# Queries and keys of ten of eighteen tiles turned by 32x32 squares on VectorE instead of by TensorE

## The chip, the cores and the metric

The kernel runs on one NeuronCore of a Trainium2 chip. The metric is the device time of one execution in microseconds (us), lower is better. The engines are written as the profile writes them: PE is TensorE (PEld its weight loads), DVE VectorE, ACT ScalarE, POOL GpSimd and SP SyncE, which here only issues DMAs.

## The reference

Three stages run one after the other on 2304 tokens (4 batches of 576), all in float32: sliding-window attention with 8 heads of 64 and a window of 64 keys, a gated layer of width 1536, and a soft mixture of 8 experts with 4 slots each.

```python
scores = (q @ k.T) / sqrt(64);  keep 0 <= i - j < 64          # per batch and head
x = softmax(scores) @ v                                        # -> [2304, 512]
x = ((x @ w_a) * (x @ w_b)) @ w_out                            # 512 -> 1536 -> 512
logits = x @ phi                                               # 32 slots
slot_in = softmax(logits, over tokens).T @ x
slot_out[e] = relu(slot_in[e] @ w1[e]) @ w2[e]                 # 8 experts
out = softmax(logits, over slots) @ slot_out
```

## The kernel before

Tokens come in 18 tiles of 128. For each tile the attention gives x in two float32r halves (a high part and a rest), and the gated layer multiplies them with w_a and w_b in three column groups. One half of one such group, (tile, group, a or b), is a slot: 12 matmuls of 128x512 into one PSUM bank, `psa` or `psb` (line 430). There are 108 slots. ACT empties `psa` (line 437), DVE multiplies `psb` with it (line 439), and each bank has one buffer, so the next slot of the same letter needs it emptied. In the steady part a tile has six slots.

All other PE work is put between and into the slots by hand: `at(n, f, ...)` puts a function at slot n, `run_slot` runs what stands there, and PE's instructions keep that order. The order of the other engines, and of the DMAs in their queues, is set by a planner that works with times of its own; what one engine has been given runs strictly in order.

The attention of tile t (for t from 5) starts at slot s = sA[t], six slots after that of the tile before in the steady part, three or four at the end (slots 80, 83 and 86 for tiles 15 to 17). The steps that matter here:

- `load` (line 193): q and k of a tile are fetched by SP into one buffer each (tags "q" and "k"), tokens on the partitions, 512 numbers each.
- `att_q` at s - 2 (line 217): four PE transposes of 128x128 into PSUM `tq`, and one ACT copy to `qTs` that also multiplies by -SCALE (line 224). `att_k` at s - 1 (line 227): a POOL copy of the last 64 keys of the tile before (line 232), four PE transposes into `tk`, one DVE copy to `kTs` (line 243; ACT for the first five tiles, line 241). `qTs` and `kTs` hold two tiles each.
- `att_s` at s (line 245): 16 float32 matmuls of 64x64 weights (queries) by 64x128 (keys), which the trace shows as 32 pairs of load and matmul (line 258). DVE adds the mask and takes the minimum (line 271), ACT takes eight exponentials (line 278).
- `att_n` and `att_pt` at s + 1 and s + 2: DVE scales the probabilities, turns them by 32x32 squares into `pq` (line 305; tiles from 6), and POOL's DMA queue writes the squares to DRAM and reads them back in order as `pT` (lines 312 and 318).
- `att_pv` at s + 6 (line 332): 32 matmuls with v (line 346), then ACT and DVE make x (lines 349 and 351).

The product g is turned in the same way for the routing (`r_b`, line 454): DVE squares into `gq` (line 457), four writes and one read in SP's queue (lines 463 and 468), then 12 matmuls (24 pairs) at line 482. `pq` and `gq` share the three buffers of tag "e". `dps` and `ups` (lines 548 and 558) are later steps of the routing. Behind the slots comes the stage of the experts, whose weights SP fetches into memory that the attention has left.

Of the kernel before, what the change touches and what calls it, by code (L numbers as in the profile page):

```python
# [11 lines left out]
F32 = mybir.dt.float32  # L12
# [3 lines left out]
ACTF = mybir.ActivationFunctionType  # L16
# [4 lines left out]
P = 128  # L21
# [36 lines left out]
BIG = 1.0e9  # L58
HUGE = 3.0e38
# [6 lines left out]
def swa_glu_softmoe_kernel(  # L66
# [13 lines left out]
    nc = tc.nc  # L80
# [5 lines left out]
    W = 64  # L86
# [7 lines left out]
    SCALE = 1.0 / float(D) ** 0.5  # L94
    EPS = 1.0e-9
    NFIRST = 4
    NLAST = 3
    NPLAIN = NFIRST + 2
    N_EX1 = 3
    N_EX2 = 7  # L100
    EARLY = 6
# [3 lines left out]
    dram = ctx.enter_context(tc.tile_pool(name="dram", bufs=1, space=bass.MemoryType.DRAM))  # L105
# [5 lines left out]
    small = ctx.enter_context(tc.tile_pool(name="small", bufs=3))  # L111
    ex1 = ctx.enter_context(tc.tile_pool(name="ex1", bufs=N_EX1))

# [23 lines left out]
    def transpose(o, i):  # L137
        nc.tensor.transpose(o, i, ident)  # L138

    def build_ident():  # L140
        nc.gpsimd.memset(ident, 0.0)
        nc.gpsimd.affine_select(
            out=ident, in_=ident, pattern=[[-1, P]], compare_op=ALU.not_equal,
            fill=1.0, base=0, channel_multiplier=1,
        )

        nc.gpsimd.memset(masks, 0.0)
        for h in range(2):
            m = masks[W * h:W * h + W]
            nc.gpsimd.affine_select(  # L150
                out=m[:, 3], in_=m[:, 3], pattern=[[-1, W]], compare_op=ALU.is_ge,
                fill=BIG, base=0, channel_multiplier=1,
            )
            nc.gpsimd.affine_select(
                out=m[:, 0:3], in_=m[:, 0:3], pattern=[[0, 3], [1, W]], compare_op=ALU.is_gt,
                fill=BIG, base=0, channel_multiplier=-1,
            )
            nc.gpsimd.memset(m[:, 1 - h], BIG)

    def build_ri():  # L160
        nc.gpsimd.memset(ri, 0.0)
# [18 lines left out]
    att = att_stack.enter_context(tc.tile_pool(name="att", bufs=2))  # L180
# [10 lines left out]
    loaded = {}  # L191
# [19 lines left out]
    sts = {}  # L211
    xts = {}

    qTs = att.tile([P, 2, 4, P], F32, name="qTs", bufs=1)
    kTs = att.tile([P, 2, 4, W + P], F32, name="kTs", bufs=1)

    def att_q(t):
        tq = ps_t.tile([P, 4, P], F32, tag="t", name="tq")
        x = loaded[t]["q"]
        for u in range(4):  # L220
            transpose(tq[:, u], x[:, 2 * u:2 * u + 2].rearrange("p h d -> p (h d)"))
        yield
        qT = qTs[:, t % 2]
        nc.scalar.activation(out=qT, in_=tq, func=ACTF.Copy, scale=-SCALE)
        sts[t] = {"qT": qT}

    def att_k(t):
        new, old = slice(W, W + P), slice(P, P + W)
        if t == 0:
            nc.gpsimd.memset(kTs[:, 0, :, 0:W], 0.0)  # L230
        else:
            nc.gpsimd.tensor_copy(kTs[:, t % 2, :, 0:W], kTs[:, (t - 1) % 2, :, old])  # L232
        yield
        tk = ps_t.tile([P, 4, P], F32, tag="t", name="tk")
        x = loaded[t]["k"]
        for u in range(4):
            transpose(tk[:, u], x[:, 2 * u:2 * u + 2].rearrange("p h d -> p (h d)"))
        yield
        k32 = kTs[:, t % 2, :, new]
        if t <= NFIRST:  # L240
            nc.scalar.copy(out=k32, in_=tk)
        else:
            nc.vector.tensor_copy(k32, tk)  # L243

    def att_s(t):
        st = sts[t]
        qT = st["qT"]
        sm = small.tile([P, 8], F32, tag="sm", name="sm")
        nmx = small.tile([P, 8], F32, tag="nmx", name="nmx")
        st["pr"], st["sm"] = [], sm  # L250

        sps = [ps_s.tile([P, 4, P], F32, tag=f"s{h}", name=f"s{h}") for h in range(2)]
        for u in range(4):
            for h in range(2):
                r = slice(W * h, W * h + W)
                for b in range(2):
                    c = slice(W * b, W * b + W)
                    nc.tensor.matmul(  # L258
                        sps[h][c, u], lhsT=qT[r, u, c], rhs=kTs[r, t % 2, u, W * b:W * b + P],
                    )  # L260
            if u % 2:
                yield
        edge = [b for b in range(2) if (2 * t + b) % NBLK == 0]
        v = 1 - edge[0] if edge else 2
        mk = masks[:, v:4:3 - v]
        for h in range(2):
            pr = att.tile([P, 4, P], F32, tag="pr", name="pr", bufs=3)
            st["pr"].append(pr)
            for u in range(4):
                i = 4 * h + u  # L270
                nc.vector.tensor_tensor_reduce(  # L271
                    out=pr[:, u].rearrange("p (a k) -> p a k", a=2), in0=sps[h][:, u].rearrange("p (a k) -> p a k", a=2), in1=mk, scale=1.0, scalar=HUGE,
                    op0=ALU.add, op1=ALU.min, accum_out=nmx[:, i:i + 1],
                )
            yield
            for u in range(4):
                i = 4 * h + u
                nc.scalar.activation(  # L278
                    out=pr[:, u], in_=pr[:, u], func=ACTF.Exp, scale=-1.0,
                    bias=nmx[:, i:i + 1], accum_out=sm[:, i:i + 1],  # L280
                )
            yield
# [15 lines left out]
    def att_pt(t, hh):  # L298
        st = sts[t]
        if t >= NPLAIN:  # L300

# [30 lines left out]
    def att_pv(t):  # L332
        st = sts[t]
        xps = ps_t.tile([P, 4, P], F32, tag="x", name="xps", bufs=1)
        for b in range(2):
            vt = loaded[t]["b" if b else "a"]
            c = slice(W * b, W * b + W)
            for u in range(4):
                for h in range(2):
                    o = xps[W * h:W * h + W, u, c]  # L340
                    if t >= NPLAIN:
                        o = o.rearrange("p (i q) -> p i q", i=2)
# [13 lines left out]
    whi, wlo = {}, {}  # L356
    wbufs = {"w0": 8, "w1": 8, "w2": 4, "w3": 4, "e": N_EX1}
    wo_dram = dram.tile([DFF, DM], F32, name="wo_dram")
# [345 lines left out]
    def use(key):  # L704
        used.add(key)
        return exw[key]
# [11 lines left out]
    def at(n, f, *a):  # L718
        events[round(2 * n)].append((f, a))
# [6 lines left out]
    sA = {}  # L726
    for t in range(NTILE - 1, NFIRST - 1, -1):
        sA[t] = min(first[t] - (8 if t >= NPLAIN else 6), sA.get(t + 1, NSLOT) - 3)
    lastA = sA[NTILE - 1] + 7
    by_squares = [t for t in range(2, NTILE - NLAST) if done[t, NFG - 1] + 2 < lastA]  # L730
    R = {}
    for t in range(NTILE - NLAST):
        R[t] = max(done[t, NFG - 1] + (3 if t not in by_squares else 4 if t == NTILE - NLAST - 1 else 5), R[t - 1] + 4 if t else 24)
    for t in range(NFIRST, NTILE):
        s = sA[t]
        at(s, att_s, t)
        at(s + 1, att_n, t, 0)
        at(s + 1, att_n, t, 1)
        at(s + 2, att_pt, t, 0)
        late = 2 if t >= NPLAIN else 0  # L740
        at(s + 2 if late else s + 3, att_pt, t, 1)
        at(s + 4 + late, att_pv, t)
        at(s - 2, att_q, t)
        at(s - 1, att_k, t)
        if t + 1 < NTILE:
            at(s, load, t + 1, "qk")
            at(s + 5 + late, load, t + 1, "ab")
    for t in range(NTILE):
        if t < NTILE - NLAST:
            r = R[t]  # L750
# [16 lines left out]
    a, b, c = LAST  # L767
# [11 lines left out]
    def open_ex():  # L779
# [3 lines left out]
        slots.extend([(p2, "as1")] * 2 + [(p2, "gT1")] * 2)  # L783
        slots.extend([(ex1, "e")] * N_EX1 + [(exs["ex2"], "y")] * N_EX2 + [(exs["ex3"], "z")] * N_EX3 + [(gp, "g"), (xp, "x")])
        slots.extend([(wp, "w0")] * 8 + [(wp, "w1")] * 8 + [(wp, "w2")] * 4 + [(xp, "x")] + [(wp, "w3")] * 4)
        slots.extend([(xp, "x")] * 2 + [(gp, "g")] * 3)
        fetch(4 + N_EX1 + N_EX2 + N_EX3)
        for t in turns.values():
# [17 lines left out]
    def run_slot(n):  # L806
# [8 lines left out]
        for _ in pieces:  # L815
            pass

    build_ident()
    SPLIT = 6 * NFIRST
    works = {  # L820
        "Ph": lambda _: run(nc.sync.dma_start, phi, moe2_phi.rearrange("(k p) s -> p k s", p=P)), "Ri": lambda _: build_ri(),
        "Tq": lambda t: load(t, "qk"), "Tv": lambda t: load(t, "ab"), "Aq": att_q, "Ak": att_k, "As": att_s, "An": att_n,
        "Ap": att_pt, "Av": att_pv, "Sa": partial(stage_w, "a"), "Sb": partial(stage_w, "b"),
        "Da": partial(split_w, "a"), "Db": partial(split_w, "b"), "Ga": lambda t, fg: glu(t, fg, "a", "a"),
# [26 lines left out]
    sps = ps_t.tile([P, KD, NS], F32, tag="x", name="sps", bufs=1)  # L851
    with tc.manual_schedule(engines=MANUAL):
# [16 lines left out]
        for h in range(2):  # L869
            c = slice(DM // 2 * h, DM // 2 * (h + 1))  # L870
# [14 lines left out]
    for u in range(2):  # L885
        hps = [ps_ab.tile([P, 512], F32, tag="ab"[n], name=f"h{n}") for n in range(2)]
        for kk in range(KD):
            for n in range(2):
                for e in range(4):
                    nc.tensor.matmul(  # L890
                        hps[n][32 * e:32 * e + 32], lhsT=sinT[:, kk],
                        rhs=use(("1", u, kk, e, n)),
# [129 lines left out]
```

## Time and profile before

| | us |
|---|---|
| median of 3 runs | 539.0 (538.02 to 540.81) |
| the profiled execution, its own time | 537.18 |
| its span, first to last instruction | 535.4 |
| PE busy | 492.5 (92%) |
| DVE busy | 315.1 (59%) |
| ACT busy | 201.3 (38%) |
| POOL busy | 120.7 (23%) |

The durations below are those of the profiled execution. Its time lies 1.8 us over its span and 1.8 us under the median. The first 150 us also decode and split the weights, chiefly on DVE; from there to 470 us run the steady slots; the rest is the experts. [...]

### The profile page before, as it was taken

The page shows a single profiled execution, that of the slowest core. Times are in us where ns is not written, and L with a number is a line of the kernel's source. Part 1 is how long each engine was busy: PE and PEld are TensorE (multiplying, and loading weights), DVE is VectorE, ACT ScalarE, POOL GpSimd, SP SyncE. Part 2 cuts the span into 40 slices and gives each one's busy share as a digit, 9 for nine tenths or more (in the row PEclk, how much of TensorE's full clock was granted, in tenths as well). Part 3 has the DMA queues.
Part 4 walks back from the last instruction along what each step waited for, and adds up shares of the span by engine and source line. Part 5 has one row for each costly group of instructions (what it writes and reads, how often), then busy time and mean ns, then how long its engine had stood idle before and what let it go on. Part 6 is the DMA issues. An engine that isn't in the chain of part 4 may idle for free.

```text
span 535.4 us, 10977 instructions
## 1 busy us (share of the span) xinstructions
PE 492.5 (92%) x4039; PEld 362.4 (68%) x4039; DVE 315.1 (59%) x897; ACT 201.3 (38%) x621; POOL 120.7 (23%) x182
## 2 busy tenths in 40 slices
PE   4479788899998999999999999999999999989992
PEld 3367566677776777787778787787777777743452
DVE  3999999896456474756647466377674211242132
ACT  5667575354444232433324233243432212141012
POOL 3555447532000212112031120313221000020000
PEclk9998999999999999999999999999999999999997
DMA  9987168647444759776676657767779899799997
GB/s 275 259 240 240 44 224 249 204 146 203 119 119 104 199 129 239 192 184 156 159 190 145 179 142 174 197 159 180 190 213 291 305 360 366 265 343 341 348 350 245
DMA packets 142102, 116.01 MB, mean 217 GB/s; under 512 B 81888, under 2 KB 122848, under 8 KB 142048
## 3 DMA queue, kind: packets, MB, share of 16 engines
q1 hardware_dynamic: 136864, 99.58, 63.6%
q0 software_dynamic: 5184, 15.73, 10.4%
q8 instruction: 32, 0.52, 0.4%
q14 instruction: 22, 0.18, 0.1%
HBM read 90.90 MB, written 24.38 MB: 215 GB/s over the span
## 4 chain that ended last, share of the span: by engine, by line
PE 74%; DVE 15%; DMA 4%; issue 3%; ACT 1%; SPq 1%; POOL 0%; POOLq 0%; ACTq 0%
PE psb L430 25%; PE psa L430 24%; PE ops L924 3%; PE xps L346 3%; PE ups L558 3%; PE lps L482 3%; DVE w L373 3%; PE h L890 2%; PE s L258 2%; DVE w L377 2%; DVE w L367 2%; DVE pr L271 2%; PE tg L138 1%; DVE w L369 1%; DMA st<-in_moe_w_b_dram 1%
## 5 line engine op out<-in xcount | busy, mean ns | idle before, releaser
L430 PE MATMUL psb<-whb,x 128*128 128x512 f32 x432 | 153.7, 407 | 2.8 <-DVE g L439 2.2
L430 PE MATMUL psa<-wha,x 128*128 128x512 f32 x432 | 152.0, 406 | 2.4 <-ACT wha L413 1.6
L430 PEld LDWEIGHTS psb<-whb,x 128*128 128x128 f32 x432 | 81.3, 188 | 30.3 <-issue 9.9
L430 PEld LDWEIGHTS psa<-wha,x 128*128 128x128 f32 x432 | 81.1, 188 | 24.1 <-issue 3.9
L430 PE MATMUL psa<-wla,x 128*128 128x512 f32 x216 | 84.5, 391 | 1.0 <-POOL wla L415 1.0
L430 PE MATMUL psb<-wlb,x 128*128 128x512 f32 x216 | 84.6, 391 | 0.9 <-POOL wlb L415 0.9
L439 DVE TENSOR_TENSOR g<-psb,g 128x512 f32<-128x512 f32 x53 | 36.5, 689 | 71.5 <-PE psb L430 68.6
L437 ACT COPY g<-psa 128x512 f32<-128x512 f32 x53 | 31.1, 586 | 92.9 <-PE psa L430 82.6
L278 ACT ACTIVATE pr<-pr,nmx 128x128 f32<-128x128 f32 x144 | 56.0, 393 | 17.7 <-DVE nmx L271 17.7
L312 POOL DMA_DIRECT2D pd<-pq x48 | 26.4, 557 | 116.8 <-DVE pq L305 86.3
L430 PEld LDWEIGHTS psa<-wla,x 128*128 128x128 f32 x216 | 40.7, 189 | 8.3 <-POOL wla L415 1.4
L430 PEld LDWEIGHTS psb<-wlb,x 128*128 128x128 f32 x216 | 40.7, 189 | 7.6 <-POOL wlb L415 1.2
L349 ACT CAST x<-xps 128x512 fp32r<-128x512 f32 x18 | 10.6, 587 | 51.3 <-PE xps L346 51.3
L258 PE MATMUL s<-kTs,qTs 64*64 64x128 f32 x576 | 23.5, 299 | 6.4 <-DVE nmx L271 3.5
L457 DVE STREAM_TRANSPOSE gq<-g 128x512 f32<-128x512 f32 x39 | 27.4, 705 | 1.2 <-DMA gd<-gq 0.6
L278 ACT ACTIVATION_READ_ACCUMULATOR pr<-pr,nmx 128x1 f32 x144 | 27.4, 190 | 0.0
L318 POOL DMA_DIRECT2D pT<-pd x24 | 18.1, 758 | 39.9 <-DMA pd<-pq 35.4
L271 DVE CUSTOM_DVE_ANT_0 pr<-s,masks 128x128 f32<-128x128 f32 x112 | 24.8, 285 | 3.3 <-PE s L258 3.3
L258 PEld LDWEIGHTS s<-kTs,qTs 64*64 64x64 f32 x576 | 18.1, 147 | 10.1 <-issue 4.7
L232 POOL COPY kTs<-kTs 128x256 f32<-128x256 f32 x17 | 8.2, 483 | 66.1 <-DVE kTs L243 61.4
L415 POOL TENSOR_TENSOR wlb<-w,whb 128x512 fp32r<-128x512 f32 x12 | 17.5, 1455 | 18.4 <-ACT whb L413 18.4
L367 DVE TENSOR_SCALAR w<-w 128x512 f32<-128x512 f32 x24 | 14.4, 602 | 10.2 <-ACT w L365 10.2
(140 smaller groups left out, 721.8 us busy)
## 6 DMA issues: line engine op xcount, KB each, us to landing
xw<-in_moe_w_dram SPq DMA_DIRECT2D x39, 512.0 KB, 6.9
xw<-in_moe_w_dram SPq DMA_DIRECT2D x50, 256.0 KB, 5.9
gd<-gq SPq DMA_DIRECT2D x156, 64.0 KB, 2.9
gT<-gd SPq DMA_DIRECT2D x39, 256.0 KB, 3.2
st<-in_moe_w_b_dram SPq DMA_DIRECT2D x12, 512.0 KB, 5.9
st<-in_moe_w_a_dram SPq DMA_DIRECT2D x12, 512.0 KB, 5.5
st<-in_moe_w_out_dram SPq DMA_DIRECT2D x12, 512.0 KB, 5.2
pd<-pq POOLq DMA_DIRECT2D x48, 128.0 KB, 3.1
```

What stands on the lines that cost most here:

```text
L258: nc.tensor.matmul(sps[h][c, u], lhsT=qT[r, u, c], rhs=kTs[r, t % 2, u, W * b:W * b + P],)
L271: nc.vector.tensor_tensor_reduce(out=pr[:, u].rearrange("p (a k) -> p a k", a=2), in0=sps[h][:, u].rearrange("p (a k) -> p a k", a=2), in1 ...
L278: nc.scalar.activation(out=pr[:, u], in_=pr[:, u], func=ACTF.Exp, scale=-1.0, bias=nmx[:, i:i + 1], accum_out=sm[:, i:i + 1],)
L312: nc.gpsimd.dma_start(out=pd[:, :, i].rearrange("j k e -> k j e"), in_=pq[32 * i:32 * i + 32].rearrange("p j h u q -> p j (h u q)"),)
L318: nc.gpsimd.dma_start(out=pT, in_=pd[:, :, :, P * h:P * h + P].rearrange("j k i e -> (j k) i e"))
L346: nc.tensor.matmul(o, lhsT=vt[:, 2 * u + h, :], rhs=r)
L367: nc.vector.tensor_scalar(out=t, in0=t, scalar1=DBL_LO, scalar2=DBL_HI, op0=ALU.max, op1=ALU.min)
L415: nc.gpsimd.tensor_tensor(out=lo, in0=w32, in1=hi.bitcast(F32), op=ALU.subtract)
L430: nc.tensor.matmul(ps, lhsT=l[:, kk], rhs=r, start=(n == 0), stop=(n == 3 * KD - 1))
L437: nc.scalar.copy(out=pas[t, fg], in_=ps)
L439: nc.vector.tensor_tensor(out=g, in0=ps, in1=pas.pop((t, fg)), op=ALU.mult)
L457: nc.vector.transpose(out=gq.rearrange("p (j c t) -> p c j t", j=4, c=4), in_=gts[t][:, 512 * fg:512 * fg + 512].rearrange("p (c j f) -> p ...
```

## The change

Tiles 8 to 17 no longer use `att_q` and `att_k`. Instead, three steps run per tile, beginning seven slots ahead of `att_s` (six for tile 8):

- `turn_qk` at r: DVE turns q and k by 32x32 squares, two instructions over 128x512, into `sq`, which takes a buffer of tag "e".
- `move_qk` at r + 1: ACT's DMA queue writes `sq` to DRAM, four DMAs of 128 KB.
- `back_qk` at r + 2.5: ACT's DMA queue reads it back, one DMA of 256 KB into `qTs` and one into `kTs`; POOL copies the 64 old keys.

The loads of q and k for these tiles are issued earlier, as soon as the tile before has been turned. For all 18 tiles the layout changes: `qTs` is now [token, head pair], so that the 64 queries of one matmul's weights stand 16 bytes apart, and `kTs` has blocks of 32 tokens, so that the 128 keys are four runs of 32. The factor -SCALE moves from ACT's copy of the queries into DVE's mask instruction, and the mask's fill is divided accordingly.

```diff
+    NTURN = NPLAIN + 2
-                fill=BIG, base=0, channel_multiplier=1,
+                fill=-BIG / SCALE, base=0, channel_multiplier=1,
...
-    qTs = att.tile([P, 2, 4, P], F32, name="qTs", bufs=1)
-    kTs = att.tile([P, 2, 4, W + P], F32, name="kTs", bufs=1)
+    qTs = att.tile([P, 2, P, 4], F32, name="qTs", bufs=1)
+    kTs = att.tile([P, 2, 6, 4, 32], F32, name="kTs", bufs=1)
...
-        nc.scalar.activation(out=qT, in_=tq, func=ACTF.Copy, scale=-SCALE)
+        nc.scalar.copy(out=qT.rearrange("p t u -> p u t"), in_=tq)
...
+    def turn_qk(t):
+        sq = ex1.tile([P, 4, 2, 4, 32], F32, tag="e", name="sq")
+        for i, nm in enumerate("qk"):
+            nc.vector.transpose(
+                out=sq[:, :, 0].rearrange("p a u j -> p a (u j)").rearrange("p a (j u) -> p u a j", u=4) if nm == "q"
+                else sq[:, :, 1].rearrange("p a u j -> p u a j"),
+                in_=loaded[t][nm].rearrange("p (u h) (e r) -> p u (h e) r", h=2, e=2),
+            )
+        sts[t] = {"sq": sq}
+
+    def move_qk(t):
+        sq = sts[t]["sq"]
+        qd = dram.tile([4, 32, 4, 2 * P], F32, tag="qd", name="qd", bufs=2)
+        for c in range(4):
+            nc.scalar.dma_start(
+                out=qd[:, :, c].rearrange("a r e -> r a e"),
+                in_=sq[32 * c:32 * c + 32].rearrange("p a i u j -> p a (i u j)"),
+            )
+        sts[t] = {"qd": qd}
+
+    def back_qk(t):
+        qd = sts[t]["qd"]
+        sts[t] = {"qT": qTs[:, t % 2]}
+        for i, x in enumerate((
+            qTs[:, t % 2].rearrange("p (c j) u -> p c (j u)", c=4), kTs[:, t % 2, 2:6].rearrange("p c u j -> p c (u j)"),
+        )):
+            nc.scalar.dma_start(out=x, in_=qd[:, :, :, P * i:P * i + P].rearrange("a r c e -> (a r) c e"))
+        old_keys(t)
...
-                        sps[h][c, u], lhsT=qT[r, u, c], rhs=kTs[r, t % 2, u, W * b:W * b + P],
+                        sps[h][c, u], lhsT=qT[r, W * b:W * b + W, u], rhs=kTs[r, t % 2, 2 * b:2 * b + 4, u],
...
-                    out=pr[:, u].rearrange("p (a k) -> p a k", a=2), in0=sps[h][:, u].rearrange("p (a k) -> p a k", a=2), in1=mk, scale=1.0, scalar=HUGE,
+                    out=pr[:, u].rearrange("p (a k) -> p a k", a=2), in0=sps[h][:, u].rearrange("p (a k) -> p a k", a=2), in1=mk, scale=-SCALE, scalar=HUGE,
...
-        at(s - 2, att_q, t)
-        at(s - 1, att_k, t)
+        if t >= NTURN:
+            r = turnA[t] = max(s - 7, sA[t - 2] - 1, sA[NTURN - 1])
+            at(r, turn_qk, t)
+            at(r + 1, move_qk, t)
+            at(r + 2.5, back_qk, t)
+            at(max(s - 11, turnA.get(t - 1, sA[NTURN - 1] - 2) + .5), load, t, "qk")
+        else:
+            at(s - 2, att_q, t)
+            at(s - 1, att_k, t)
+            at(sA[t - 1] if t > NFIRST else s - 6, load, t, "qk")
         if t + 1 < NTILE:
-            at(s, load, t + 1, "qk")
```

## Rows read from the trace of the kernel before

**Rows 1.** The page: busy time of each engine, share of the span, instructions.

```profile
PE 492.5 (92%) x4039; PEld 362.4 (68%) x4039; DVE 315.1 (59%) x897; ACT 201.3 (38%) x621; POOL 120.7 (23%) x182
```

**Rows 2.** Stretches of 20 us: length, busy us of each engine, PE clock, DMA share, GB/s.

```profile
170.00:190.00 20.00, 20.00 (x120) 15.39 (x118) 11.34 (x32) 6.15 (x24) 4.15 (x7) 1.00 0.67 180
...
290.00:310.00 20.00, 20.00 (x174) 15.78 (x173) 10.80 (x38) 6.22 (x24) 4.10 (x7) 1.00 0.72 181
...
470.00:490.00 20.00, 17.43 (x145) 7.38 (x140) 7.19 (x34) 6.11 (x23) 4.40 (x14) 1.00 1.05 342
```

**Rows 3.** Timeline of PE, one tile: start us, us, engine, line, operation, tiles, count.

```profile
282.85 0.64 PE L346 MATMUL xps<-pT,ldb 128*64 128x64 f32 x16
...
283.42 1.10 PE L258 MATMUL s<-kTs,qTs 64*64 64x128 f32 x32
...
284.45 0.86 PE L482 MATMUL lps<-gT,wphi 128*32 128x128 f32 x24
...
285.24 0.50 PE L430 MATMUL psa<-wha,x 128*128 128x512 f32 x1
...
291.19 0.48 PE L430 MATMUL psa<-wha,x 128*128 128x512 f32 x1
...
296.76 0.60 PE L138 MATMUL tq<-ident,ldq 128*128 128x128 f32 x4
...
297.19 0.27 PE L138 MATMUL dps<-ident,e 128*128 128x128 f32 x1
...
299.84 0.39 PE L430 MATMUL psa<-wha,x 128*128 128x512 f32 x1
...
300.07 0.60 PE L138 MATMUL tk<-ident,ldk 128*128 128x128 f32 x4
...
300.60 0.85 PE L558 MATMUL ups<-g,dt 128*32 128x384 f32 x8
...
304.02 0.39 PE L430 MATMUL psb<-whb,x 128*128 128x512 f32 x1
...
304.33 0.69 PE L346 MATMUL xps<-pT,lda 128*64 128x64 f32 x16
```

**Rows 4.** Tiles tq and tk, 195 to 390 us: duration ns min/median/max, first and last start.

```profile
L138 PE MATMUL tq<-ident,ldq x40: 270/272/273, 205.8 to 381.7; 128*128 128x128 f32 x40
L138 PE MATMUL tk<-ident,ldk x40: 270/272/328, 209.2 to 385.3; 128*128 128x128 f32 x40
L224 ACT ACTIVATE qTs<-tq x10: 584/600/602, 206.5 to 382.1; 128x512 f32<-128x512 f32 x10
L243 DVE COPY kTs<-tk x10: 691/691/692, 209.9 to 385.7; 128x512 f32<-128x512 f32 x10
```

**Rows 5.** The chain that ended last, tile 0: start us, us, what.

```profile
146.96 0.79 PE lps L482 x24
```

**Rows 6.** Timeline of ACT, the same tile as in the timeline of PE.

```profile
288.30 0.59 ACT L437 COPY g<-psa 128x512 f32<-128x512 f32 x1
```

**Rows 7.** Timeline of POOL's DMA queue; in brackets the wait before it and for what.

```profile
296.21 1.50 POOL L318 DMA_DIRECT2D pT<-pd  x2 [3.26 <-DMA pd<-pq]
```

**Rows 8.** DMA queues and issues: first two of 170 to 350 us, last of 400 to 470.

```profile
q0 software_dynamic: 2816, 8.39, 17.7%
...
pT<-pd POOLq DMA_DIRECT2D x16, 256.0 KB, 3.6
...
pT<-pd POOLq DMA_DIRECT2D x2, 256.0 KB, 5.5
```

**Rows 9.** Timeline of SP's DMA queue.

```profile
292.63 2.11 SPq L463 DMA_DIRECT2D gd<-gq  x4
```

**Rows 10.** Groups by line: xcount, busy us, mean ns, idle before and its releaser.

```profile
L457 DVE STREAM_TRANSPOSE gq<-g 128x512 f32<-128x512 f32 x39 | 27.4, 705 | 1.2 <-DMA gd<-gq 0.6
L365 ACT ACTIVATE w<-st 128x512 f32<-128x512 f32 x24 | 16.1, 675 | 8.6 <-DMA st<-in_moe_w_b_dram 5.0 <-POOL wlb L415 1.8 <-PE pp L589 1.2
L413 ACT CAST wha<-w 128x512 fp32r<-128x512 f32 x12 | 7.4, 620 | 11.9 <-DVE w L377 11.9
```

More of the change, by code (lines that the diff above doesn't have):

```diff
@@ L155, in build_ident @@
                 out=m[:, 0:3], in_=m[:, 0:3], pattern=[[0, 3], [1, W]], compare_op=ALU.is_gt,
-                fill=BIG, base=0, channel_multiplier=-1,
+                fill=-BIG / SCALE, base=0, channel_multiplier=-1,
             )
-            nc.gpsimd.memset(m[:, 1 - h], BIG)
+            nc.gpsimd.memset(m[:, 1 - h], -BIG / SCALE)
     def build_ri():
@@ L223, in att_q, with old_keys @@
         qT = qTs[:, t % 2]
-        nc.scalar.activation(out=qT, in_=tq, func=ACTF.Copy, scale=-SCALE)
+        nc.scalar.copy(out=qT.rearrange("p t u -> p u t"), in_=tq)
         sts[t] = {"qT": qT}
-    def att_k(t):
[L228 to L232, printed above, removed]
+    def old_keys(t):
+        if t == 0:
+            nc.gpsimd.memset(kTs[:, 0, 0:2], 0.0)
+        else:
+            nc.gpsimd.tensor_copy(kTs[:, t % 2, 0:2], kTs[:, (t - 1) % 2, 4:6])
+    def att_k(t):
+        old_keys(t)
         yield
@@ L238, in att_k @@
         yield
-        k32 = kTs[:, t % 2, :, new]
+        k32 = kTs[:, t % 2, 2:6].rearrange("p c u j -> p u c j")
+        tk = tk.rearrange("p u (c j) -> p u c j", c=4)
         if t <= NFIRST:
@@ L243, in att_k @@
             nc.vector.tensor_copy(k32, tk)
+    def turn_qk(t):
[23 more added lines that the diff above has]
+            nc.scalar.dma_start(out=x, in_=qd[:, :, :, P * i:P * i + P].rearrange("a r c e -> (a r) c e"))
+        old_keys(t)
     def att_s(t):
@@ L733, in swa_glu_softmoe_kernel @@
         R[t] = max(done[t, NFG - 1] + (3 if t not in by_squares else 4 if t == NTILE - NLAST - 1 else 5), R[t - 1] + 4 if t else 24)
+    turnA = {}
     for t in range(NFIRST, NTILE):
@@ L742, in swa_glu_softmoe_kernel @@
         at(s + 4 + late, att_pv, t)
-        at(s - 2, att_q, t)
-        at(s - 1, att_k, t)
+        if t >= NTURN:
[4 more added lines that the diff above has]
+            at(max(s - 11, turnA.get(t - 1, sA[NTURN - 1] - 2) + .5), load, t, "qk")
+        else:
+            at(s - 2, att_q, t)
+            at(s - 1, att_k, t)
+            at(sA[t - 1] if t > NFIRST else s - 6, load, t, "qk")
         if t + 1 < NTILE:
-            at(s, load, t + 1, "qk")
             at(s + 5 + late, load, t + 1, "ab")
```

## The prediction

> **What bounds the kernel now.** Read the page first: PE is busy for 92% of the span, DVE for 59%, ACT for 38% [rows 1]. An average says little about the place of the change, so the table by stretches comes next. The steps that are removed run from 206 to 385 us [rows 4], and in that region PE is busy for 20.00 of every 20 us; the fifteen stretches from 170 to 470 us look alike save the one from 450, at 19.68, and two of them are shown. DVE is at 11 and ACT at 6 of 20 there, and the granted clock is 1.00, its upper level [rows 2]. So PE's own work is the bound, not a wait, and work taken off PE there comes off the time, as long as nothing new makes PE wait. Behind 470 us PE is at 17.43 of 20 and the DMA engines at 1.05 [rows 2]. That stage starts its fetches by slots that PE has finished, all behind the removed steps, so it should move forward whole.
>
> **What comes off PE.** The timeline shows one tile. `tq` starts at 296.76 and the next transpose, `dps`, at 297.19: without `tq` it would stand at 296.76, which is 0.43 us. The last `psa` matmul ahead of `tk` starts at 299.84 and `ups` behind it at 300.60, 0.76 us later. Where such a group follows a matmul directly, it starts 0.31 us later (304.02 to 304.33). So `tk` costs 0.45 us, and both 0.88 us per tile [rows 3]. There are 40 transposes of each kind in the region, ten tiles [rows 4]: 10 x 0.88 = 8.8 us. This is all PE work, in a stretch without PE idle time, so I count it in full.
>
> **What comes off the others.** One ACT copy (0.60 us) and one DVE copy (0.69 us) per tile [rows 4]. Neither engine is the bound, so I count nothing.
>
> **DVE's squares.** Two turns per tile at 0.705 us each [rows 10], against 0.69 saved: 0.72 us more per tile. For q the output steps by 16 bytes, which no turn in this trace does; from no change to twice the time, the addition is 0.72 to 1.4 us. A tile takes six slots, about 22 us (from the second half of `xps` at 282.85 to the first half of the next at 304.33 is 21.5 [rows 3]), and DVE is idle for some 9 of 20 us [rows 2]. That idle time hides it; without it the ten tiles would cost 7 to 14 us. I count 0.
>
> **ACT's DMAs.** Each tile now has six issues in ACT's stream. The nearest rows are SP's: four issues in 2.11 us, 0.53 each [rows 9], so 2.1 us for the writes and 1.1 for the reads. ACT's stream is strictly in order, so behind the writes it waits for DVE's turn if that is late, and behind the reads it waits until the writes have landed. POOL's queue does the same with squares of the same size and stood 3.26 us for it [rows 7]. Queued behind that are ACT's copies out of `psa`, the exponentials and x. PE waits for the copy: it ended at 288.89 and PE needed the bank at 291.19, so it may come 2.3 us late [rows 3, 6]. The writes alone (2.1) fit. Wait and reads together are 3.3 + 1.1 = 4.4 us, 2.1 too many where they begin just as an `a` slot ends. Two of a tile's three `a` slots have so little room (behind the third stand `ups` and other PE work), so blocks starting in 2 x 2.1 of 22 us hurt, 19%, with a mean excess of 1.05 us: 0.2 us per tile, 2.0 for ten. The bounds are 0 (always covered) and 10 x 2.1 = 21 us; I take 1.8, since the planner can put other ACT work ahead of the reads.
>
> **The strided weights.** In `att_s` the 64 weight columns of a matmul now stand 16 bytes apart, in all tiles. No weight load in the trace is strided, so I bound it. The 32 pairs take 1.03 us (283.42 to 284.45); four run side by side (two head halves, two token halves), so a round takes 0.129 us. The second half of `xps` loads as much per partition and round, two loads of 64 columns, and does its eight rounds in 0.57 us, 0.071 each [rows 3]. A load that takes no longer than now costs nothing. At half speed a round is 0.142 us at most, 0.013 x 8 = 0.10 us per tile, and 1.4 us over the 13 tiles from 5 on, where PE is the bound. At quarter speed it is 0.284 us: 0.155 x 8 = 1.24 us per tile, 16.1 us. Between 0 and 1.4 I take 0.5; 16.1 stays as a rival. [...] The keys are now four runs of 32. The routing's matmuls read such runs already, and their 24 pairs take 0.79 us (284.45 to 285.24), as those of tile 0 did, whose g was turned by PE and lies in one run [rows 3, 5]. So that is free.
>
> **Start.** For tiles 0 to 7 ACT's copy of the queries writes with steps of 16 bytes. The nearest row is an ACT operation that reads with steps of 8 bytes, 675 ns against 620 [rows 10]. Five such copies lie in the startup, where ACT and DVE work ahead of PE: from 0 to 5 x 0.6 = 3.0 us if each doubled and all were on the path. I take 0.3, since one step costs 0.06 us by those rows. The factor moved into the mask instruction is a constant that it had already: 0.
>
> **More DMA traffic.** POOL's queue moves the squares of the probabilities, equal in size; for eight tiles it took 17.7% of the DMA engines from 170 to 350 us [rows 8]. Ten tiles would add 22% to a share of about 0.7 [rows 2], so transfers get slower. The tightest user is `att_pv`: the second `pT` read was issued at 296.96 (half of 1.50 us behind 296.21 [rows 7]), lands 3.6 us later [rows 8], at 300.6, and is used at 304.33 [rows 3]: 3.8 us to spare. That time holds the next tile's `tq` and `tk`, so it shrinks to 2.9. On the busy engines behind 400 us a `pT` read took 5.5 us [rows 8], 1.9 more, which fits. I count 0. [...]
>
> **The sum.** 537.18 - 8.8 + 0.5 + 0.3 + 1.8 = 531.0 us in the profiled execution's terms. That execution lies 1.8 us under the median, so I forecast 532.8 us.
>
> **Rivals.**
> 1. ACT's wait takes the place of the transposes: the block of 4.4 us falls on the end of an `a` slot in half of the tiles. 5 x 2.1 = 10.5 in place of 1.8: 539.7, as a median 541.5. If it does so in all ten: 550.2, 552. For it speaks that the planner's times are not the chip's; against it, the 18 us (4.5 slots) between the reads and `att_s`, which let it choose.
> 2. Strided weights at quarter speed, the case on the other side: 537.18 - 8.8 + 16.1 + 0.3 + 1.8 = 546.6, as a median 548.4. It decides from 8.8 / 13 = 0.68 us per tile on, a round of 0.214 us, three times the 0.071 of `xps`. For it: nothing strided has been tried here. Against it: half speed nearly disappears behind the matmuls.
> 3. Traffic reaches `att_pv`: writes and `pT` reads both take 1.9 us longer, 3.8 against 2.9 to spare, and PE stands 0.9 us per tile. 537.18 - 8.8 + 0.5 + 0.3 + 9 = 538.2, as a median 540.0. Exponentials held up by ACT's issues would push the same way.
>
> **How the numbers follow.** 0.5% is 2.7 us, about what a measurement of this kernel can tell from no change. Forecast 0.66, its own range 528.5 (no cost but the transposes, and a little run difference) to 535.5. Rival 1: 0.10 for half of the tiles, which counts as no change, and 0.04 for all, slower. Rival 2: 0.10, slower. Rival 3: 0.10, no change. So faster 0.66, same 0.20, slower 0.14, and the range is 528.5 to 541.5.
>
> **What would show it.** Right: no `tq` and `tk` behind 200 us, PE busy still 20.00 of 20, and `att_s` to `att_s` some 0.9 us less than 22. ACT's wait: PE idle ahead of `psa`, released by ACT's copy. Strided weights: the 1.03 us of `att_s` grows. Traffic: PE idle ahead of `xps`, released by a DMA. I am wrong if PE's freed time shows up as PE waits, or if `att_s` grows by 0.68 us.

## The result and the profile after

The changed kernel is slower: 546.39 us median of four runs (543.66 to 547.74) against 538.99. The ratio worked out from the single runs is 1.0123, with an interval of [1.0078, 1.0167]; the two medians alone give 1.0137. The profiled execution took 543.66 us, 6.5 us more than that of before. The forecast was 532.8, the range ended at 541.5. Runs more than 1.5% above the fastest of their kernel count as slow and are left out of the times below: 546.18 in the first set of the row of ten chunks, and 548.47 and 549.85 (with POOL's copy) and 545.17 (with the row of chunks) in the two kernels with the full traffic added.

The same stretches as in [rows 2], after (length, busy us of each engine, PE clock, DMA share, GB/s), and that of 370 to 390 us:

```profile
170.00:190.00 20.00, 20.00 (x120) 15.64 (x121) 11.44 (x29) 6.10 (x21) 4.14 (x7) 1.00 0.63 171
290.00:310.00 20.00, 18.94 (x114) 14.59 (x114) 11.86 (x33) 5.51 (x24) 4.10 (x7) 1.00 0.91 231
...
370.00:390.00 20.00, 18.07 (x154) 13.60 (x151) 11.51 (x51) 7.72 (x34) 5.61 (x9) 0.91 0.88 241
...
470.00:490.00 20.00, 17.38 (x140) 9.76 (x142) 9.38 (x36) 6.75 (x23) 3.88 (x12) 1.00 0.92 311
```

Ahead of the change's tiles and behind the slots PE is as busy as before (20.00, and 17.38 against 17.43). Between them PE is no longer full: 18.94 of 20 us where it was 20.00, while the DMA engines' share rose from 0.72 to 0.91. Near 380 us the granted clock is 0.91 too: for 3.4 us, behind waits of 0.83 and 1.11 us at `xps`, it stood at 0.50 in place of 1.00, and the 24 pairs of `lps` took 1.51 us where they took 0.86.

What PE waited for between 190 and 400 us, after (us in total, times, longest); the kernel before has no line for `xps` in the same list:

```profile
PE xps L383 <- DMA pT<-pd: 9.7, 10, 2.1
PE ups L595 <- DVE dt L587: 0.9, 1, 0.9
```

The timeline of PE at the end of one tile, after, which answers to [rows 3]:

```profile
303.65 0.39 PE L467 MATMUL psa<-wha,x 128*128 128x512 f32 x1
303.97 0.85 PE L595 MATMUL ups<-g,dt 128*32 128x384 f32 x8
...
307.39 0.39 PE L467 MATMUL psb<-whb,x 128*128 128x512 f32 x1
308.29 0.33 PE L383 MATMUL xps<-pT,lda 128*64 128x64 f32 x2 [0.52 <-DMA pT<-pd]
309.16 0.62 PE L383 MATMUL xps<-pT,lda 128*64 128x64 f32 x13 [0.54 <-DMA pT<-pd]
...
309.63 0.68 PE L383 MATMUL xps<-pT,ldb 128*64 128x64 f32 x15
310.24 1.24 PE L295 MATMUL s<-kTs,qTs 64*64 64x128 f32 x32
311.41 0.86 PE L519 MATMUL lps<-gT,wphi 128*32 128x128 f32 x24
```

`tk` is gone: from the last `psa` matmul to `ups` it is 0.32 us, where it was 0.76, so 0.44 less, as forecast. But `xps`, due 0.3 us behind the `psb` matmul at 307.39, stops twice for `pT`. And `att_s` takes 1.17 us (310.24 to 311.41) where it took 1.03.

I matched the starts of the same PE instructions in both traces and followed how far the later kernel lags. Over the ten tiles the lag shrinks by 8.8 us at the places of `tq` and `tk`. It grows by 12.1 us at `xps` of six tiles (3.7 for tile 7, 2.0, 1.5, 1.8 and 0.8 for tiles 8, 11, 12 and 13, 2.5 for tile 14; more than the 9.7 of the list, since the matmuls then come in pieces), by 0.14 in each `att_s`, 1.8 for 13 tiles, by 0.9 at the one `ups` that waits for `dt`, and by 0.7 where the clock is low: -8.8 + 12.1 + 1.8 + 0.9 + 0.7 = 6.7, against 6.5 between the two executions.

Where `pT` loses its time shows on POOL's queue, first the reads of tile 7 before, then tiles 7, 11 and 14 after (in brackets the wait before and for what):

```profile
205.49 1.50 POOL L318 DMA_DIRECT2D pT<-pd  x2 [3.60 <-DMA pd<-pq]
```
```profile
201.40 2.20 POOL L349 DMA_DIRECT2D pd<-pq  x4 [11.81 <-DVE l L529]
209.98 0.41 POOL L233 COPY kTs<-kTs 128x256 f32<-128x256 f32 x1 [6.39 <-DMA kTs<-qd]
210.59 1.50 POOL L355 DMA_DIRECT2D pT<-pd  x2 [0.20 <-issue]
...
295.48 0.40 POOL L233 COPY kTs<-kTs 128x256 f32<-128x256 f32 x1 [15.00 <-DMA kTs<-qd]
295.96 2.20 POOL L349 DMA_DIRECT2D pd<-pq  x4
302.57 1.50 POOL L355 DMA_DIRECT2D pT<-pd  x2 [4.41 <-DMA pd<-pq]
...
364.19 2.20 POOL L349 DMA_DIRECT2D pd<-pq  x4 [0.76 <-DVE pq L342]
372.50 0.40 POOL L233 COPY kTs<-kTs 128x256 f32<-128x256 f32 x1 [6.11 <-DMA kTs<-qd]
373.11 0.76 POOL L355 DMA_DIRECT2D pT<-pd  x1 [0.21 <-issue]
```

The copy of the old keys (L233) now waits for ACT's read of the keys of the tile before, and what is queued behind it on POOL waits with it. In tile 7 the writes of the squares are issued by 203.60; the reads of them follow at 210.59, 7.0 us later, because the copy stood ahead of them, while the kernel before had 3.60. In tile 14 it is 6.7 us (before: 4.0). At 295.48 the copy stood ahead of the writes. And behind those, where nothing stood in the way, the reads still waited 4.41 us for the writes ([rows 7]: 3.26).

How much of the 12.1 us hangs on the copy can be estimated from the trace: in each tile I compare the issue that stood behind the copy with the moment when its data were there (squares made, or writes landed). The copy put it off by 2.4, 1.1, 0.7, 1.2, 0 and 3.3 us in the six tiles. As tile 14 lost only 2.5, that is about 8 us. The rest are later landings, and squares that DVE finished later: 1.2, 2.1 and 1.6 us later behind the start of `att_s` than before, in tiles 7, 8 and 14.

The DMAs of 170 to 350 us, after (queue: packets, MB, share of the 16 engines; issue: count, KB each, median us to landing), against [rows 8]:

```profile
q0 software_dynamic: 2688, 7.99, 16.5%
q10 hardware_dynamic: 11851, 7.73, 15.0%
...
pT<-pd POOLq DMA_DIRECT2D x16, 256.0 KB, 5.7
...
kTs<-qd ACTq DMA_DIRECT2D x7, 256.0 KB, 5.6
```

ACT's new queue (q10) takes 15.0% of the engines, and a `pT` read lands in 5.7 us instead of 3.6.

So there are two candidates, which may work together: POOL's queue, held by the copy, and the traffic, which makes landings later.

### The profile page after: what moved, and what is told of

The parts are those of the page before. It is cut to its first block, busy times and chain, and to the rows that moved or that the text cites. A ratio compares the mean times of both kernels' runs of the same rounds, so it can differ in the third digit from the quotient of the medians.

```text
span 541.9 us, 10921 instructions
## 1 busy us (share of the span) xinstructions
PE 491.5 (91%) x3959; PEld 361.5 (67%) x3959; DVE 322.8 (60%) x907; ACT 198.6 (37%) x611; POOL 120.8 (22%) x182
## 4 chain that ended last, share of the span: by engine, by line
PE 53%; DVE 18%; DMA 18%; issue 5%; ACT 3%; POOL 2%; SPq 1%; ACTq 0%; POOLq 0%; DVEq 0%
PE psb L467 16%; PE psa L467 16%; DMA pT<-pd 5%; DMA kTs<-qd 5%; PE ops L969 3%; DVE w L410 3%; PE xps L383 3%; PE h L935 2%; DVE w L414 2%; DMA pd<-pq 2%; PE lps L519 2%; DVE w L404 2%; DVE pr L308 2%; PE s L295 2%; DMA gd<-gq 2%
## 5 line engine op out<-in xcount | busy, mean ns | idle before, releaser
L233 POOL COPY kTs<-kTs 128x256 f32<-128x256 f32 x17 | 8.2, 483 | 123.9 <-DMA kTs<-qd 51.1
L295 PE MATMUL s<-kTs,qTs 64*64 64x128 f32 x576 | 25.9, 315 | 7.0 <-DVE nmx L308 3.3
L295 PEld LDWEIGHTS s<-kTs,qTs 64*64 64x64 f32 x576 | 21.4, 207 | 10.6 <-DVE nmx L308 3.7
L383 PE MATMUL xps<-pT,lda 128*64 128x64 f32 x288 | 16.5, 245 | 11.7 <-DMA pT<-pd 9.7
L383 PEld LDWEIGHTS xps<-pT,lda 128*64 128x64 f32 x288 | 12.7, 151 | 19.8 <-DMA pT<-pd 12.2
```

The costliest lines, as they stand in the source:

```text
L295: nc.tensor.matmul(sps[h][c, u], lhsT=qT[r, W * b:W * b + W, u], rhs=kTs[r, t % 2, 2 * b:2 * b + 4, u],)
L383: nc.tensor.matmul(o, lhsT=vt[:, 2 * u + h, :], rhs=r)
```

## The experiments

Each time is a median beside runs of the kernel before on the same chip (538.5 to 539.3 us); ratios are to those, with their interval.

**The layouts alone.** All tiles keep their transposes on PE; only the layouts of queries and keys, and the factor in the masks, are those of the changed kernel.

```diff
-    NTURN = NPLAIN + 2
+    NTURN = 18
```

> The changed kernel with NTURN = 18: every tile keeps its eight PE transposes, so only the new layout of qTs and kTs, the strided copy of the queries and the moved factor are left. Both theories (POOL's queue holds the squares back; the traffic makes landings late) say the same here: no PE idle time ahead of xps, att_s 0.12 us longer in each of the 13 tiles from 5 on (1.6 us) and about 0.5 us in the startup, so some 541.1 us against 539.0. If the layout alone costs over 5 us, both theories are wrong on where the time went.

Measured: 541.27 us, 1.0047 [1.0024, 1.0071], and no wait at `xps`. The weight loads of `att_s` (duration ns, minimum, median, maximum), first the kernel before, then this one:

```profile
L258 PEld LDWEIGHTS s<-kTs,qTs x316: 129/133/133, 214.5 to 389.9; 64*64 64x64 f32 x158
```
```profile
L295 PEld LDWEIGHTS s<-kTs,qTs x312: 188/206/217, 194.9 to 383.1; 64*64 64x64 f32 x156
```

A load with steps of 16 bytes takes 206 ns in place of 133, and most of that hides: 0.14 us per tile, 1.8 of the 2.5 us between the medians. The forecast had 0.5, and 1.4 as the bound. It is a real cost, but not the result.

**Traffic that nobody uses, added to the kernel before**, first alone, then with a POOL copy that reads what came back.

```diff
+        nc.scalar.dma_start(out=qd[:, :, c]..., in_=flat[...].to_broadcast([32, 4, 4 * W]))    # x4
+        nc.scalar.dma_start(out=spare[:, i], in_=qd[...])                                      # x2
+        nc.gpsimd.tensor_copy(spare[:, 0, 0:2], spare[:, 1, 0:2])                              # second kernel only
```

> The kernel before, with the traffic of the change added and nothing else: for tiles 8 to 17 ACT's queue writes 512 KB of a constant to DRAM in four DMAs and reads them back in two into a spare buffer of tag e, at the slots of the change. No result depends on it and q and k go through PE as before. Theory of POOL's queue: nothing waits, 539 to 540.5 us. Theory of the traffic: pT lands over 5 us after its issue, PE idles 3 to 10 us ahead of xps in all, and the time is 542 to 549 us.

> The kernel before with an added 512 KB written and read back per tile in ScalarE's queue for tiles 8 to 17, which nothing in the computation uses (the earlier run of this gave 541.75 without a wait at xps), and now one GpSimd copy per tile that reads what came back, at the place where the changed kernel's copy of old keys stands. GpSimd's queue: this copy waits for the read, holds pd and pT, and waits of several us at xps appear, time 544 to 551. Traffic: the copy changes nothing, no wait at xps, 541 to 542.5.

Measured: 541.75, 1.0047 [1.0024, 1.0071], and 544.59, 1.0113 [1.0097, 1.0129]. Neither tells much. The added writes depend on nothing, so the planner put many of them ahead of 190 us, and between 170 and 350 us ACT's queue took only 8.8% and 7.7% of the engines, half of the change's 15.0% (a `pT` read landed in 3.6 and 4.6 us). In the second kernel most of the lag, 4.8 us, is there by 147 us. Only tile 14 had a wait at `xps` (1.5 us), behind the new copy. Their place was wrong, and an added load must depend on the data whose load it imitates.

**The old keys' copy behind the writes.** The copy is issued on POOL behind the four `pd` writes of the tile before. In the first kernel the tiles 15 and 16 then read old keys that are already overwritten; in the second the copies of tiles 15 to 17 stay where the change has them.

```diff
-        old_keys(t)                      # second kernel: stays for t >= 15
+    def late_keys(t):
+        with tc.issue_after(sts[t - 1]["pd"]):    # the last of the four pd writes
+            old_keys(t)
...
+            at(s - 1, late_keys, t)          # second kernel: only for t < 15
```

> The changed kernel with one thing moved: POOL's copy of the 64 old keys is queued behind the pd writes of the tile before, by when the keys it reads have long landed. Traffic and ACT's issues are as in the changed kernel. Theory of POOL's queue: the copy no longer waits for ACT's read of kTs ahead of the pd and pT issues, PE idle time ahead of xps falls from 12 us to under 2, and the time is about 539.0 - 8.8 + 1.6 + 0.5 = 532.3 us. Theory of the traffic: pT still lands after 5.8 us instead of 3.6, most of the idle time ahead of xps stays, and the time is 541 to 546 us.

> The kernel after, with GpSimd's copy of the old keys of tiles 8 to 14 issued only behind the four pd DMAs of the tile before, as in the earlier run, but the copies of tiles 15 to 17 left where the changed kernel has them, so that nothing is copied from keys already overwritten and tile 15's scores do not wait. If GpSimd's queue is the cause (the copy waits for ScalarE's read of the keys and holds pd and pT behind it): of the 12 us of waits at xps for pT, those of tiles 8 to 14 shrink to a few us (the earlier run left 3.7 in all), and the time is 536.5 to 539. If the traffic by itself is the cause (pT lands 2.2 us later because the DMA engines are fuller): the waits stay at about 12 us and the time at 545 to 547.

Measured: 541.24, 1.0042 [1.0009, 1.0075], and 539.25, 1.0011 [0.9992, 1.0030]. The waits of 190 to 400 us, first kernel, then second:

```profile
PE s L298 <- POOL kTs L233: 4.7, 1, 4.7
PE xps L386 <- DMA pT<-pd: 2.3, 3, 1.0
```
```profile
PE xps L388 <- DMA pT<-pd: 3.0, 5, 1.1
```

The wait at `xps` falls from 9.7 to 2.3 and 3.0 us. The first kernel pays 4.7 us in another place: in the last tiles, three or four slots apart, the copy behind the writes is too late for `att_s`. Without that, 7.1 us of the changed kernel are back (546.39 against 539.25; the slowest of the ten runs took 540.90, the fastest of the changed kernel's four 543.66). This is the cleanest comparison here: in the two traces the instructions of DVE, SP and, the copies apart, POOL stand in the same order, and those of ACT but for one write. What stays is a kernel as fast as before, not 6 us faster.

**No copy on POOL from tile 9 on.** The keys stand in a row of ten chunks, two old ones and two tiles of four. An odd tile finds its old keys in place; an even tile's come by a further 128 KB read in ACT's queue.

```diff
-    kTs = att.tile([P, 2, 6, 4, 32], F32, name="kTs", bufs=1)
+    kTs = att.tile([P, 10, 4, 32], F32, name="kTs", bufs=1)
...
-        old_keys(t)
+        if t == NTURN:
+            old_keys(t)
+        if t % 2:
+            nc.scalar.dma_start(out=kTs[:, 0:2]..., in_=qd[:, :, 2:4, P:2 * P]...)
...
-            at(r + 2.5, back_qk, t)
+            at(max(r + 2.5, sA[t - 1] + .5), back_qk, t)
```

> The kernel after with no copy of old keys on GpSimd from tile 9 on: the keys stand in a row of ten 32-key chunks, two old and two tiles of four, so that an odd tile finds its old keys where the even tile before it left them, and an even tile's come by a third read (64 KB) in ScalarE's queue from the same copy in DRAM. The DMA traffic is that of the changed kernel and a little more. GpSimd's queue: no instruction on GpSimd waits for ScalarE's reads any more, the waits at xps fall under 4 us, time 535 to 539. Traffic: the waits stay near 12 us, 545 to 548. If the late reads of tiles 15 to 17 (now behind the scores of the tile before) are too late, a wait at these scores shows, up to 4 us.

(In the text above the further read is given as 64 KB; it is 128.)

> The kernel with the row of ten chunks once more, unchanged, for a second profile and more times: all of the changed kernel's traffic, no copy of old keys on GpSimd. Both theories expect the time of the earlier run, 535.5, and in the profile 3 to 5 us of waits at xps for pT: what the traffic does when nothing holds GpSimd's queue.

Measured: 535.09 us, 0.9935 [0.9911, 0.9958], in the first set (three runs, 533.95 to 535.86), and 539.42, 1.0000 [0.9968, 1.0033] in the second (ten runs, 535.26 to 542.69). The kernel is the same and the intervals don't meet, so an interval doesn't cover what changes from one set to the next, and a difference of 4 us between kernels of different sets isn't settled by their intervals alone. The second profile has 2.0 us of waits at `xps`, less than the 3 to 5 expected, and another wait (PE's wait at `xps` of 190 to 400 us; timelines of DVE, then of PE):

```profile
PE xps L389 <- DMA pT<-pd: 2.0, 3, 1.2
```
```profile
363.87 0.71 DVE L500 STREAM_TRANSPOSE gq<-g 128x512 f32<-128x512 f32 x1 [3.93 <-DMA gd<-gq]
...
368.49 0.28 DVE L593 COPY dt<-dps 128x128 f32<-128x128 f32 x1
```
```profile
368.83 1.51 PE L601 MATMUL ups<-g,dt 128*32 128x384 f32 x8 [2.65 <-DVE dt L593]
```

`gq` shares its three buffers with `pq` and now `sq`. DVE stood 3.93 us until DMAs out of an earlier `gq` had landed and a buffer was free; the copy of `dt`, queued behind, came late, and PE waited 2.65 us for it. PE's clock was lower then: the granted clock of 360 to 380 us is 0.83, and `ups` took 1.51 us, against 0.85 in the change's profile. A fourth buffer was not tried.

**Keys alone, half of the traffic.** Only the keys go by squares; queries keep their transposes and whole runs of weights. One kernel has the row of ten chunks, the other POOL's copy as in the changed kernel.

```diff
-        for i, nm in enumerate("qk"):
-            nc.vector.transpose(...)
+        nc.vector.transpose(out=sq.rearrange("p a u j -> p u a j"), in_=loaded[t]["k"]...)
...
-                        sps[h][c, u], lhsT=qT[r, W * b:W * b + W, u], ...
+                        sps[h][c, u], lhsT=qT[r, u, W * b:W * b + W], ...
...
+            at(s - 2, att_q, t)
```

> The same row of chunks, but only the keys of tiles 8 to 17 are turned by squares; queries are transposed on TensorE with the layout of the kernel before, so weights are read in whole runs. Against the kernel before it takes away 10 transposes of 0.44 us and adds half of the changed kernel's traffic. GpSimd's queue: no waits at xps to speak of, 539 - 4.4 = 534.5, range 533.5 to 536. Traffic: half of the 12 us of waits, 539 - 4.4 + 6 = 540.5.

> Keys alone by squares as in the kernel of 533.45, but the old keys copied by GpSimd, where the changed kernel has that copy, in place of the row of ten chunks: half of the changed kernel's traffic, with the copy that waits for ScalarE's read. GpSimd's queue: the copy still stands ahead of pd or pT in some tiles, and waits at xps of 2 to 8 us come back, 536 to 541. Traffic: half of it left no wait at xps in the other kernel, so none here, 533 to 534.

Measured: 533.45, 0.9906 [0.9888, 0.9925], with the row of chunks; 533.69, 0.9912 [0.9882, 0.9943], with POOL's copy. Neither has a wait at `xps`; in the first, `tk`'s 0.44 us per tile comes off in full. The second speaks against my first theory: the copy is there, waits for the same read, and costs nothing that can be told. POOL's queue and two lines of the DMAs of 170 to 350 us, keys alone with the copy:

```profile
265.51 0.40 POOL L233 COPY kTs<-kTs 128x256 f32<-128x256 f32 x1 [9.98 <-DMA kTs<-qd]
270.85 2.20 POOL L346 DMA_DIRECT2D pd<-pq  x4 [4.94 <-DVE pq L339]
276.23 1.50 POOL L352 DMA_DIRECT2D pT<-pd  x2 [3.19 <-DMA pd<-pq]
```
```profile
pT<-pd POOLq DMA_DIRECT2D x16, 256.0 KB, 4.7
...
kTs<-qd ACTq DMA_DIRECT2D x8, 256.0 KB, 4.6
```

The read is back before its time: the copy is done 4.9 us ahead of the writes that it would hold. The theory became: the copy holds POOL's queue only when the keys land late, and full traffic makes them land late.

"Late" is more than a slower transfer, though. From the end of the keys' turn on DVE to the landing of their read took 8.2 to 12.3 us here (median 10.3) and 13.3 to 21.7 in the changed kernel (17.3), while the read by itself, from issue to landing, took 4.9 and 6.0 (medians). Most of the difference comes ahead of the read's issue, where the changed kernel has twice the bytes to write, the queries' read ahead of that of the keys, and ACT's own work between. In one tile of it (9) the writes had landed at 218.34, and the read of the keys went out 5.6 us later, behind eight exponentials (ACT, after):

```profile
220.61 0.57 ACTq L279 DMA_DIRECT2D qTs<-qd  x1
...
223.59 0.39 ACT L315 ACTIVATE pr<-pr,nmx 128x128 f32<-128x128 f32 x1
...
223.93 0.53 ACTq L279 DMA_DIRECT2D kTs<-qd  x1
```

So "full traffic" below stands for the longer trip of the keys as a whole, and the experiments don't take it apart.

**Both kernels with the full traffic.** The squares of the keys are made and written twice, and the unneeded half is read to a place in DRAM ahead of the keys.

```diff
-        sq = ex1.tile([P, 4, 4, 32], F32, tag="e", name="sq")
+        sq = ex1.tile([P, 4, 2, 4, 32], F32, tag="e", name="sq")
...
+        rest = dram.tile([P, 4, P], F32, tag="rest", name="rest", bufs=2)
+        nc.scalar.dma_start(out=rest, in_=qd[:, :, :, 0:P].rearrange("a r c e -> (a r) c e"))
```

> Keys alone by squares with GpSimd's copy of the old keys, the kernel of 533.7 without a wait at xps, and now with the changed kernel's whole traffic: the squares of the keys are made and written to DRAM twice (512 KB per tile), and a read of the unneeded half goes ahead of the read of the keys in ScalarE's queue, to a scratch place in DRAM that nothing reads. TensorE's transposes of the queries stay. Theory now: GpSimd's copy holds pd and pT only when ScalarE's read of the keys lands late, and that it does under the full traffic; so waits of 5 to 12 us at xps come back, 539 to 547. Rival: the waits of the changed kernel came from what TensorE lost (its transposes gone, PV of a tile due 0.8 us earlier), and with the queries' transposes left there is none, 533 to 535.

> The same full traffic, added in the same way to the kernel with keys alone and the row of ten chunks, where nothing on GpSimd waits for ScalarE's read (533.5 with half of the traffic). Theory now: what the traffic does by itself, pT landing up to 2 us later, leaves 0 to 5 us of waits at xps, 533.5 to 538.5, and at least 3 us less than the kernel with GpSimd's copy and the same traffic. Rival, in which the copy does not matter: both have the same time within 1.5 us.

Measured: 543.81 and 537.59 with the copy (two runs, too few and too far apart for an interval), and 539.68, 0.9995 [0.9970, 1.0020], with the row of chunks (nine runs, 534.93 to 540.44). The profiled executions took 543.81 and 538.07. POOL's queue and the waits of 190 to 400 us with the copy, then the waits with the row of chunks:

```profile
232.46 0.40 POOL L233 COPY kTs<-kTs 128x256 f32<-128x256 f32 x1 [20.44 <-DMA kTs<-qd]
232.94 2.20 POOL L349 DMA_DIRECT2D pd<-pq  x4
```
```profile
PE xps L383 <- DMA pT<-pd: 6.0, 6, 1.9
```
```profile
PE xps L389 <- DMA pT<-pd: 0.5, 2, 0.3
```

The waits at `xps` are back in this profile although the queries' transposes are still there, and with all these transposes gone and no copy there were 2.0 us of them; so they don't come from what PE lost. The times don't settle it: the middle of the two with the copy, 540.7, is 1.0 us above the row of chunks, inside the 1.5 us of the rival in which the copy does not matter. The medians side by side, in us:

| | half of the traffic | full traffic, added | full traffic, queries by squares |
|---|---|---|---|
| old keys by POOL's copy | 533.69 | 540.7 (537.59 and 543.81) | 546.39 (the change itself) |
| POOL's copy behind the writes, to tile 14 | not run | not run | 539.25 |
| row of ten chunks | 533.45 | 539.68 | 535.1 and 539.4 |

With half of the traffic the copy costs nothing that can be told (0.2 us). With all of it its price is best read from the change itself, where it alone was moved: 7.1 us. The profiles with the added traffic agree (5.7 us between the executions, 5.5 between their waits at `xps`), though their kernel's times scatter too much to say so. Without the copy the step from half to full traffic is 6.2 us, and that isn't all traffic: the added kernel also turns the keys twice on DVE. In the two profiles with the row of chunks I find 3.4 us between 190 and 390 us in steps of 0.3 to 0.8, and 2.1 us ahead of 147 us, before any of the added DMAs. There the granted clock of 110 to 125 us was 0.89 in one and 1.00 in the other, for a reason that I could not find.

**Queries alone**, the opposite half, with the changed kernel's layouts:

```diff
-            at(max(s - 11, turnA.get(t - 1, sA[NTURN - 1] - 2) + .5), load, t, "qk")
+            at(max(s - 11, turnA.get(t - 1, sA[NTURN - 1] - 2) + .5), load, t, "q")
+            at(s - 1, att_k, t)
+            at(sA[t - 1], load, t, "k")
```

> The changed kernel with the queries alone turned by squares; the keys of tiles 8 to 17 go through PE and DVE as before, so POOL's copy waits for DVE and not for a read in ACT's queue, and the added traffic is half. Theory of POOL's queue: no idle time ahead of xps, 539.0 - 4.4 + 1.6 + 0.5 = 536.7 us. Theory of the traffic: about half of the 12 us of idle time stays, 540 to 543 us.

Measured: 536.15, 0.9958 [0.9929, 0.9986], without a wait at `xps`. Half of the traffic again, and POOL's copy reads keys that PE and DVE made. It is 2.7 us behind keys alone; the strided weights account for 1.8. Its profile has one wait of 1.7 us, at `dps`: DVE stood 3.38 us for a shared buffer ahead of the turn of the queries, and ACT's `ce`, which `dps` waits for, came late behind it.

The fastest kernels are the two with keys alone, 0.9% under the kernel before.

## Why the prediction was wrong

**The failing step is "More DMA traffic".** It ended with "I count 0", since a landing 1.9 us later fits into 2.9 us. The size of that one landing was right (3.6 to 5.7, and I had allowed 5.5). The room was read too wide: 3.6 is a median over both reads of a tile, and in the tile shown the second took 4.3, which leaves 3.1 us and not 3.8. Two more things were left out. First, `pT` isn't one landing: the writes of the squares, then the reads, stand in a row, and both got later. Rival 3 says so (1.9 twice against 2.9), with 0.9 us per tile, and had a chance of 0.10. Its place was right, its price 9 us; measured were 12.1, but with the copy's hold in it, and with the copy moved 3.0 us of waits were left. Second, POOL's copy of the old keys. The prediction takes `att_k` apart into transposes and a DVE copy, and never names its first instruction, which moves to `back_qk`, behind ACT's read. That made POOL's queue wait for ACT's, and the `pd` and `pT` DMAs of another tile with it. Nothing in the sum or the rivals carries that, and it is worth 7.1 us (546.39 against 539.25 with the copy moved).

**What comes off PE**: right, 8.8 us, as 0.44 for each of twenty groups.

**The strided weights**: mechanism right, size off. 0.14 us per tile against a bound of 0.10; 1.8 us against 0.5. Rival 2 (1.24 us per tile) did not happen. I took the second half of `xps` as the price of plain loads and let the doubled load hide behind it; the loads grew by only half (133 to 206 ns) and yet showed more than the upper of my bounds.

**Start**: counted at 0.3 from a step of 0.06 us per copy. With the layouts alone a copy of the queries with 16-byte steps takes 1.08 us in place of 0.60, so the step is 0.48. What the startup pays for it isn't shown: PE's lag is 0.5 us at 150 us in the change's profile, but two kernels that are alike up to there differ by 2.1 (keys alone and full traffic added, both with the row of chunks).

**ACT's DMAs**: counted at 1.8, measured 0 where the prediction looked. Among PE's waits of 190 to 400 us there is none at `psa`, so rival 1 did not happen either. It asked only what waits behind ACT's issues, and not how long the issues stand behind ACT's work; there the keys' read lost time (5.6 us in the tile shown above), and the copy with it.

**DVE's squares**: counted at 0, measured 0.9 in the change's profile (PE's one wait for `dt`, which DVE made behind both turns, after 0.92 us of waiting for a shared buffer). The idle time of DVE was there, but the buffers of tag "e" were not priced: DVE's wait for one cost PE 2.65 us in one profile of the row of chunks and 1.7 with queries alone. The turn of the queries, with its strided output, takes 1085 ns against 688 for the keys', inside my bounds (groups by line, 195 to 390 us, after: xcount, busy us, mean ns, idle before):

```profile
L254 DVE STREAM_TRANSPOSE sq<-ldq 128x512 f32<-128x512 f32 x9 | 9.8, 1085 | 1.2 <-DMA gd<-gq 0.9 <-DMA ldq<-in_q_dram 0.3
...
L254 DVE STREAM_TRANSPOSE sq<-ldk 128x512 f32<-128x512 f32 x9 | 6.2, 688 | 2.5 <-DMA ldk<-in_k_dram 2.5
```

**The sum** with the measured terms: 537.18 - 8.8 + 1.8 + 12.1 + 0.9 + 0.7 = 543.9, and the execution took 543.66.

## What to carry to other kernels

When a step moves, list all of its instructions and walk each one's queue: a 0.4 us copy on an idle engine cost nothing until it had to wait for a late transfer, and then it held the DMAs queued behind it. A round trip through DRAM is a chain of issues and landings (for the keys in the changed kernel 17.3 us from turn to landing, 6.0 of them the read; medians); price the whole chain, with the landing times of the fuller engines (5.7 us for a `pT` read here, and not 3.6) and with the work that its issues stand behind, not one link. Where one cost depends on another (the copy costs 0.2 us with half of the traffic and 7.1 with all of it), test the combinations before naming a cause, and move one thing at a time.

## What was not expected of the hardware

- A weight load with columns 16 bytes apart takes 206 ns in place of 133, half more and not a multiple, and a 32x32 turn with such an output 1085 ns in place of 688.
- With ACT's queue taking 15.0% of the DMA engines, a 256 KB read landed in 5.7 us instead of 3.6, at a share of 0.91 against 0.72 in the stretch shown.
- A wait of 2.65 us came with a granted clock of 0.83 over 360 to 380 us, which is 6.8 us at 0.50, the lower clock that the change's profile shows. The `ups` behind it took 1.51 us in place of 0.85, so the stall cost more than itself. Not each wait does so: in the change's profile waits of 2.15 and 1.11 us at `xps` of tile 7 left the clock at 1.00.
